# Attention block on one core: transposed maxima issued one value block sooner in the program, and the row-sum reciprocals one key tile later

## The chip, the cores and the metric

The kernel runs on one core of a Trainium2 chip. The metric is device time in microseconds for one execution; lower is better. The unchanged kernel took 2012.49 us, the median of 3 runs (2010.25 to 2014.61).

## What is computed

A transformer block: pre-norm multi-head attention with 32 heads of 20 channels over 2048 tokens of width 640, and then a gated feed-forward block. The change lies in the attention alone. Cut to that:

```python
scores = jnp.einsum("bhqd,bhkd->bhqk", q, k) * (Dh ** -0.5)
p = _softmax(scores, axis=-1)
o = jnp.einsum("bhqk,bhkd->bhqd", p, v)
h = x + o.transpose(0, 2, 1, 3).reshape(B, S, D) @ wo
h2 = h + _B_ref(_layernorm(h, axis=-1), w_gate, w_up, w_down)
```

## The kernel before, in words

The kernel has three stages: layer norm with the projections to queries, keys and values (until about 319 us in the trace), attention (until about 1443 us), and the feed-forward part. The attention is cut into 32 **units** u = 0 to 31: a group of 4 heads (g = u // 4) and a chunk of 512 queries (c = u % 4). A unit has 16 **key tiles** kt of 128 keys, so the loop runs 512 **steps**, numbered now = 16 u + kt.

A step's order is written out by hand as a string, `ORDER = "WhSmsSHMs"`, and every engine executes its own instructions in the order of the program:

- `s`, `S` (four in a step): one score product of a head on the tensor engine (PE, L1328) into a PSUM bank `ps_one`, then its exponential on ACT (L1334) into `probs`. Four banks serve `ps_one` in turn, so a bank comes round again after four uses.
- `W`: the **value block** (L1338), four products of the probabilities of two steps ago with the values, into one accumulator `acc`. Behind it stand the calls that were put off to this step (the table `later`), and one piece of `preparing`, work on the feed-forward weights (POOL copies and subtractions, loads and stores on SP; skipped at kt 3 and 4).
- `m`, `M`, `h`, `H`: score products of a *later* unit (L272), of which DVE takes the row maxima (L292, L307). The softmax subtracts these maxima inside the score product, as two extra rows of `q_stk`, so the first score product of a unit waits until the maxima have landed there.

When a unit's maxima are all there, `max_all` reduces them on DVE to `neg` (L315). How they get into `q_stk` depends on the unit. For unit 1 and the last unit of each group (v = 3, 7, ..., 31), nine times in all, `max_finish` follows: a PE transpose (L347) into a `ps_one` bank, an ACT copy and a DVE subtraction that split it in two (L89, L90), and four DMAs on SP (L354, `q_stk<-m`). For the others, POOL splits `neg` (L323, L324), DVE transposes it 4 steps later (L331), SP stores it (L332, `m_d<-turned`), and 2 steps after that SP loads it (L342, `q_stk<-m_d`).

The end of unit u - 1 lies in unit u: the last value block at kt 1, an ACT copy of the accumulator (L1348), four small DMAs that spread the row sums (L1351, `r<-o`); at the end of kt 4 the **reciprocals** on DVE (L1359), their store (L1361, `r_d<-r`) and a broadcast load of 256 KB (L1367, `rb<-r_d`); at the end of kt 9 the product `o * rb` on POOL (L1373), at the end of kt 11 four stores (L1376, `o_d<-o`). In the last two units these are earlier (kt 3, 6 and 7). At the end of kt 6 SP loads the queries of unit u + 3 (L176, `q_stk<-q_d`), and in units with c = 1 the keys, with c = 2 the values of the next group, at the end of kt 8, 10, 12 and 14 (L176, `k_stk<-k_d`; L193, `v_stk<-v_d`).

Nearly all DMAs of the attention are issued by SP, in program order. Each is given the next of eight semaphores in turn, and waits for the DMA that had it before: a DMA on SP is issued only when the eighth before it has landed.

Of the kernel before, what the change touches and what calls it, by code (L numbers as in the profile page):

```python
# [44 lines left out]
def tile_block(ctx: ExitStack, tc: tile.TileContext, x, wqkv, wo, wg, wu, wd, out):  # L45
# [42 lines left out]
    def split(src, hi, lo, lo_engine=nc.vector):  # L88
        nc.scalar.activation(hi, src, AF.Copy)  # L89
        lo_engine.tensor_tensor(out=lo, in0=src, in1=hi.bitcast(F32), op=ALU.subtract)  # L90
# [221 lines left out]
    def max_all(u):  # L312

        ends[u] = stk.tile([P, G * TPC], F32, name="neg", tag="neg", bufs=2)
        nc.vector.tensor_reduce(  # L315
            ends[u], mxs[u].rearrange("p b h t k -> p (b h t) k"), axis=AX.X, op=ALU.max, negate=True
        )
# [26 lines left out]
    def max_finish(u):  # L344

        m = (ps_one if u else ps_max)()[: G * TPC, :P]
        nc.tensor.transpose(m, ends.pop(u), ident)  # L347
        parts = stk.tile([G * TPC, 2, P], F32R, name="m2", tag="m2", bufs=1)
        split(m, parts[:, 0], parts[:, 1], nc.vector)
        for b in range(2):  # L350
            for i in range(2):
                row = b * ROW + NPART + i
                first = b * 2 * TPC
                nc.sync.dma_start(  # L354
                    queries[u][row : row + 1].bitcast(F32).rearrange(
                        "r j (t p) -> r (j t) p", t=TPC
                    ),
                    parts[first : first + 2 * TPC, i, :].bitcast(F32),
                )
# [938 lines left out]
    def weight_rings():  # L1298
        def unit(f, i):
            return lambda t: (t.rearrange("p i k n -> p (i k n)"), w_d[f][:, i])  # L1300

        def last(f):
            n = 2 if f < NF - 1 else 1
            return lambda t: (
                t[:, :, :n], w_d[f][:, 7].rearrange("p (i k n) -> p i k n", i=2, k=2)[:, :, :n]
            )

        units = stay.tile([P, 8, 2, 2, P], F32R, name="units", tag="first")
        lasts = stay.tile([P, 3, 2, 2, P], F32R, name="lasts", tag="second")
        plan = [  # L1310
            unit(f, i) for _, f in ELEMENTS for i in (range(7) if f < NF - 1 else (0, 2))
        ]
        return (
            Ring([units[:, i] for i in range(8)], plan),
            Ring([lasts[:, i] for i in range(3)], [last(f) for _, f in ELEMENTS]),
        )
# [6 lines left out]
    def scores(u, kt, j, probs):  # L1323

        p, b = divmod(j, 2)
        rows = slice(b * ROW, b * ROW + NPART + 2)
        ps = ps_one()
        nc.tensor.matmul(  # L1328
            ps,
            keys[u // NC][rows, p, kt * P : (kt + 1) * P],  # L1330
            queries[u][rows, p, :],
            start=True, stop=True,
        )
        nc.scalar.activation(probs[p][:, b, :], ps, AF.Exp, scale=scale)  # L1334
# [45 lines left out]
    todo, tail, accs, later, full, now = [], [], {}, {}, [], [0]  # L1380
    left = {u: sum(2 for a in rest if a[0] == u) for u in range(1, NU)}

    whole, halves_of = [], []

    def counted(u, n):
        left[u] -= n
# [3 lines left out]
    def next_max(b):  # L1390
        if not whole and rest:
            a = rest.pop(0)
            whole.extend((*a, i) for i in (b, 1 - b))
        if whole:
            a = whole.pop(0)
            max_one(*a)
            counted(a[0], 1)

    def next_half(b):

        if not halves_of and rest:
            a = rest.pop(0)
            halves_of.extend((i, a, []) for i in range(2))
        if not halves_of:
            return
        i, a, banks = halves_of[0]
        if not banks:
            banks.append(ps_max())
            max_half(banks[0], i, *a, b)
        else:  # L1410
            nc.tensor.keepalive_nop([nc.tensor.lower_ap(banks[0])])
            max_half(banks[0], i, *a, b)
            max_halves(banks[0], i, *a)
            counted(a[0], 2 * i)
            halves_of.pop(0)

    def weigh_next():
        u, kt, probs = todo.pop(0)
        if kt == 0:
            accs[u] = psum.tile([P, CH], F32, name="acc", tag=f"ps_{last % 3}")  # L1420
        weigh(u, kt, probs, accs[u])
        if kt == NT - 1:
            queues = [nc.sync] if u + 1 < NU else [nc.scalar, nc.sync]
            tail.append((u, *row_sums(accs.pop(u), *queues)))
# [6 lines left out]
    for u in range(NU):  # L1431
        g, c = divmod(u, NC)
        if g == NG - 1 and c >= 2:
            _, first, ln, flips, _ = ahead
            extra = [*first, *ln, lambda: None, *flips]
        for kt in range(NT):
            now[0] = u * NT + kt
            probs = [pp.tile([P, 2, CH], F32, name="probs") for _ in range(2)]
            heads = [[0, 2], [1, 3]]
            for op in ORDER if rest or whole or halves_of else LAST_ORDER:  # L1440
                if op in "mM":
                    next_max(int(op == "M"))
                elif op in "hH":
                    next_half(int(op == "H"))
                elif op in "sS":
                    scores(u, kt, heads[op == "S"].pop(0), probs)
                else:
                    if len(todo) == 2:
                        weigh_next()
                    for f in later.pop(now[0], ()):  # L1450
                        f()
                    if extra:
                        extra.pop(0)()
                    if preparing and u and kt not in (3, 4):
                        preparing.pop(0)()
                    if now[0] == (NU - NC) * NT + 8:
                        unit_ring, last_ring = weight_rings()
                        unit_ring.fill()
                        last_ring.fill()
            todo.append((u, kt, probs))  # L1460
            for v in full:
                max_all(v)
                if v % NC == NC - 1 or v == 1:
                    later.setdefault(now[0] + 2, []).append(lambda v=v: max_finish(v))
                else:
                    max_parts(v)
                    later.setdefault(now[0] + 4, []).append(lambda v=v: max_turn(v))
                    later.setdefault(now[0] + 6, []).append(lambda v=v: max_load(v))
            full.clear()
            if kt == 6 and u + 3 < NU:  # L1470
                load_queries(u + 3)
            if kt == 10 and u == 0:
                fill_ones(k_stk[1])
            if kt >= 8 and kt % 2 == 0 and c == 1 and g + 1 < NG:
                load_keys(g + 1, slice((kt - 8) // 2 * CH, (kt - 6) // 2 * CH))
            if kt >= 8 and kt % 2 == 0 and c == 2 and g + 1 < NG:
                load_values(g + 1, (kt - 8) // 2 * TPC, (kt - 6) // 2 * TPC)

            sooner = u >= NU - 2
            if kt == (3 if sooner else 4) and tail:  # L1480
                reciprocals(u - 1, tail[0][2], nc.sync)
                rb = spread(u - 1, nc.sync)
            if kt == (6 if sooner else 9) and tail:
                store_o(u - 1, tail[0][1], rb, nc.gpsimd, None)
            if kt == (7 if sooner else 11) and tail:
                store_o(u - 1, tail.pop()[1], rb, None, nc.sync)
            if g == NG - 1 and c >= 1:
                at = 8 if sooner else NT - 4
                if kt == at:
                    ahead = projection(  # L1490
                        c - 1, ps_max if c < NC - 1 else (lambda: ps_b())
                    )
                if kt in (at, at + 1, 12 if sooner else 14):
                    ahead[0][min(kt - at, 2)]()
                    if kt == at + 1 and c < NC - 1:
                        ahead[4]()
            k = 2 * (u - NU + 8)
            if kt in (12, 13) and 0 <= k + kt - 12 < ND:
                if k + kt == 12:
                    assert not preparing  # L1500
                    wo_hi = pc.tile([P, ND, D], F32R, name="wo_hi", bufs=1)
                    wo_lo = pc.tile([P, ND, D], F32R, name="wo_lo", bufs=1)
                load_wo(k + kt - 12)
            if kt in (2, 3) and 0 <= k + kt - 4 < ND:
                split_wo(k + kt - 4)
# [566 lines left out]
```

## Time and profile before

| | |
|---|---|
| median of 3 runs | 2012.49 us |
| the profiled execution | 2012.87 us, of which the span in the profile 2010.4 us |
| granted TensorE clock, mean | 0.999 |
| PE, ACT, DVE, POOL busy over the span | 99%, 72%, 80%, 39% |
| exponentials, L1334 | 2048, 612 ns each |
| reciprocals, L1359 | 32, median 243 ns |
| transposes of `max_finish` in the attention, L347 | 9, 277 ns each |

A row of the timeline gives the start, the length, the engine, the line, the operation with its output and input, and how many instructions were merged into it (a value block is eight records, two for each product); in brackets, how long the engine had been idle and what ended that. SPq stands for SP's issuing of DMAs: its length is the issue alone, not the transfer. The profile puts a wait for several semaphores down to the one that came last by its records.

### The profile page before, as it was taken

The numbers are of one execution on the slowest core, as the hardware profiler recorded it, in microseconds if no ns is written. First come the engines' busy times: TensorE is split into PE (matmuls) and PEld (weight loads), VectorE is DVE, ScalarE is ACT, GpSimd is POOL, SyncE is SP. The second block draws the span as 40 slices with busy tenths as digits, with TensorE's granted clock in tenths as the row PEclk, the third lists the DMA queues.
The fourth block names the chain that finished last, engine by engine and source line by source line (L and its number), as shares of the span: only waits on it lengthen the run. The fifth ranks groups of instructions, "written<-read, shape, count | busy, mean of one in ns | idle before, by whom it ended". The sixth has DMA issues, their size and how long they took to land. (4 is left out here: it accounts for less than half of the span.)

```text
span 2010.4 us, 41923 instructions
## 1 busy us (share of the span) xinstructions
PE 1985.1 (99%) x14794; PEld 1268.7 (63%) x14794; DVE 1599.5 (80%) x2831; ACT 1440.1 (72%) x2827; POOL 789.4 (39%) x1182
## 2 busy tenths in 40 slices
PE   8999999999999999999999999999999999999998
PEld 6999995444444444444444444455598888888887
DVE  5687778899999899998999999975477666676667
ACT  4678778999999999999999999987633222212221
POOL 7464424343453443443400011011155544844465
PEclk9999999999999999999999999999999999999999
DMA  7887563443634544435412132222268655974642
GB/s 244 255 258 257 183 206 78 128 140 105 193 103 141 152 135 138 157 127 175 150 60 68 40 86 58 79 63 62 62 215 278 228 168 174 359 248 160 203 146 93
DMA packets 199350, 310.48 MB, mean 154 GB/s; under 512 B 53744, under 2 KB 87856, under 8 KB 198120
## 3 DMA queue, kind: packets, MB, share of 16 engines
q1 hardware_dynamic: 192552, 284.21, 44.0%
q0 software_dynamic: 6496, 23.60, 4.0%
q8 instruction: 120, 1.97, 0.4%
q14 instruction: 86, 0.70, 0.1%
q10 hardware_dynamic: 96, 0.00, 0.0%
HBM read 208.11 MB, written 99.19 MB: 153 GB/s over the span
## 5 line engine op out<-in xcount | busy, mean ns | idle before, releaser
L1334 ACT ACTIVATE probs<-ps_one 128x512 f32<-128x512 f32 x2048 | 1056.1, 612 | 46.7 <-PE ps_one L1328 37.2
L292 DVE TENSOR_REDUCE mx<-ps_max 128x1 f32<-128x512 f32 x980 | 671.8, 686 | 90.6 <-PE ps_max L272 88.0
L272 PEld LDWEIGHTS ps_max<-k_stk,q_stk 60*128 60x128 f32 x1964 | 294.2, 185 | 462.8 <-DVE mx L307 393.5
L1328 PE MATMUL ps_one<-q_stk,k_stk 62*128 62x512 f32 x2048 | 570.4, 427 | 2.7 <-DMA q_stk<-m 1.8
L272 PE MATMUL ps_max<-k_stk,q_stk 60*128 60x256 f32 (+1 forms) x1964 | 565.5, 376 | 2.5 <-DVE mx L292 1.2
L1338 PE MATMUL acc<-probs,v_stk 128*32 128x512 f32 x4096 | 546.1, 605 | 0.1
L307 DVE TENSOR_REDUCE mx<-ps_max 128x2 f32<-128x512 f32 x492 | 335.8, 683 | 0.4 <-PE ps_max L272 0.4
L1328 PEld LDWEIGHTS ps_one<-q_stk,k_stk 62*128 62x128 f32 x2048 | 304.9, 184 | 15.0 <-ACT probs L1334 11.3
L1750 DVE TENSOR_TENSOR tmp<-ps_a,tmp 128x512 f32<-128x512 f32 x208 | 141.3, 690 | 122.2 <-PE ps_a L1535 96.6
L262 DVE TENSOR_REDUCE mx<-ps_max 128x2 f32<-128x512 f32 x288 | 180.8, 685 | 63.7 <-PE ps_max L240 60.2
L252 ACT ACTIVATE ps_max<-ps_max 128x512 f32<-128x512 f32 x288 | 151.6, 583 | 42.9 <-PE ps_max L240 40.3
L1629 PE MATMUL ps_b<-halves,yp 128*128 128x320 f32 x1032 | 179.0, 308 | 1.5 <-DMA halves<-j_d 1.3
L1629 PEld LDWEIGHTS ps_b<-halves,yp 128*128 128x128 f32 x1032 | 165.2, 188 | 17.5 <-POOL yp L90 1.5
L1535 PE MATMUL ps_a<-t,units 128*128 128x512 f32 x624 | 162.5, 396 | 0.0
L1338 PEld LDWEIGHTS acc<-probs,v_stk 128*32 128x32 f32 x4096 | 80.7, 108 | 128.1 <-issue 119.9
L90 POOL TENSOR_TENSOR yp<-y,yp 128x256 fp32r<-128x256 f32 x96 | 60.2, 628 | 189.7 <-ACT yp L89 189.7
L1535 PE MATMUL ps_a<-z,units 128*128 128x512 f32 x516 | 133.8, 394 | 0.0
L1535 PEld LDWEIGHTS ps_a<-t,units 128*128 128x128 f32 x624 | 112.6, 188 | 18.5
L1373 POOL TENSOR_TENSOR o<-o,rb 128x512 f32<-128x512 f32 x31 | 39.8, 1284 | 194.2 <-DMA rb<-r_d 60.6
L1634 DVE TENSOR_TENSOR h<-ps_b,h 128x320 f32<-128x320 f32 x248 | 110.1, 482 | 6.8 <-PE ps_b L1629 5.4
L671 PE MATMUL ps_one<-z_hi,w_lo 64*128 64x512 f32 x380 | 113.4, 392 | 0.0
L671 PE MATMUL ps_one<-z_lo,w_hi 64*128 64x512 f32 x380 | 112.1, 392 | 0.0
(228 smaller groups left out, 2746.5 us busy)
## 6 DMA issues: line engine op xcount, KB each, us to landing
units<-w_d SPq DMA_DIRECT2D x186, 256.0 KB
w_d<-stage SPq DMA_DIRECT2D x106, 256.0 KB
halves<-j_d SPq DMA_DIRECT2D x70, 320.0 KB
j_d<-stage SPq DMA_DIRECT2D x42, 320.0 KB
k_stk<-k_d SPq DMA_DIRECT2D x64, 160.0 KB
q_stk<-q_d SPq DMA_DIRECT2D x64, 160.0 KB
raw<-k_d SPq DMA_DIRECT2D x62, 160.0 KB
raw<-q_d SPq DMA_DIRECT2D x54, 160.0 KB
```

Source lines behind the costliest of these rows:

```text
L252: nc.scalar.activation(ps, ps, AF.Relu)
L262: nc.vector.tensor_reduce(mx[:, b, :, t, kc], ps.rearrange("p (j n) -> p j n", j=2), axis=AX.X, op=ALU.max,)
L272: nc.tensor.matmul(ps, queries[u][rows, pair, t * P : (t + 1) * P], keys[u // NC][rows, pair, k0:k1], start=True, stop=True, skip_group_ch ...
L292: nc.vector.tensor_reduce(mx[:, b, pair, t, kc : kc + 1], ps, axis=AX.X, op=ALU.max)
L307: nc.vector.tensor_reduce(max_slots(u)[:, :, pair, t, slot], ps.rearrange("p (j n) -> p j n", j=2), axis=AX.X, op=ALU.max,)
L671: nc.tensor.matmul(ps, a[rows], b[rows], start=(i == n == 0), stop=(i == 1 and n == last), skip_group_check=True,)
L1328: nc.tensor.matmul(ps, keys[u // NC][rows, p, kt * P : (kt + 1) * P], queries[u][rows, p, :], start=True, stop=True,)
L1334: nc.scalar.activation(probs[p][:, b, :], ps, AF.Exp, scale=scale)
L1338: nc.tensor.matmul(acc[32 * j : 32 * j + 32, :], values[u // NC][:, kt, j * VW : j * VW + 32], probs[j // 2][:, j % 2, :], start=(kt == 0) ...
L1535: nc.tensor.matmul(ps.rearrange("p (t n) -> p t n", t=TPC), w[k][:, i], z[k][:, :, j], start=(first and m == 0), stop=(last and m == len(n ...
L1629: nc.tensor.matmul(ps, a, b, start=(n == 0), stop=(n == len(pairs) - 1))
L1750: add = lambda out, ps, x: nc.vector.tensor_tensor(out=out, in0=ps, in1=x, op=ALU.add)
```

## The change

Two edits in the step loop. First, `max_finish` is no longer put into the table for the `W` of two steps after the maxima were complete, where it stood behind the value block. It goes into a list that is emptied at the end of the next step, so its transpose, copy, subtraction and four DMAs come ahead of the following value block. Second, in units 1 to 29 the reciprocals, their store and the broadcast load come at the end of kt 5 and not of kt 4. The products and stores that use them stay at kt 9 and 11.

```diff
-    whole, halves_of = [], []
+    whole, halves_of, behind_step = [], [], []
...
             todo.append((u, kt, probs))
+            while behind_step:
+                behind_step.pop(0)()
             for v in full:
                 max_all(v)
                 if v % NC == NC - 1 or v == 1:
-                    later.setdefault(now[0] + 2, []).append(lambda v=v: max_finish(v))
+                    behind_step.append(lambda v=v: max_finish(v))
                 else:
...
             sooner = u >= NU - 2
-            if kt == (3 if sooner else 4) and tail:
+            if kt == (3 if sooner else 5) and tail:
                 reciprocals(u - 1, tail[0][2], nc.sync)
                 rb = spread(u - 1, nc.sync)
```

On PE, around the first transpose (for unit 1, in step 13 of unit 0; L1338 is the value block, L347 the transpose, L1328 scores, L272 products for maxima), the program before has:

```order
L1328 MATMUL ps_one<-q_stk,k_stk_125 128x512 x2
L272 MATMUL ps_max<-k_stk_125,q_stk 128x256
L272 MATMUL ps_max<-k_stk_125,q_stk 128x512
L1328 MATMUL ps_one<-q_stk,k_stk_125 128x512
L1338 MATMUL acc<-probs,v_stk_126 32x512 x4
L347 MATMUL ps_one<-ident,neg 16x128
L272 MATMUL ps_max<-k_stk_125,q_stk 128x256
```

and the changed one:

```order
L1328 MATMUL ps_one<-q_stk,k_stk_125 128x512 x2
L272 MATMUL ps_max<-k_stk_125,q_stk 128x256
L272 MATMUL ps_max<-k_stk_125,q_stk 128x512
L1328 MATMUL ps_one<-q_stk,k_stk_125 128x512
L347 MATMUL ps_one<-ident,neg 16x128
L1338 MATMUL acc<-probs,v_stk_126 32x512 x4
L272 MATMUL ps_max<-k_stk_125,q_stk 128x256
```

Only the transpose and the value block change places; so it is for eight of the nine. The ninth (unit 31) moves ahead of four score products as well, and there the ACT copy also moves ahead of other work. ACT is otherwise unchanged, and POOL's order is unchanged throughout.

On SP, in unit 9, from the row-sum DMAs to the load of the next unit's maxima (w_d is a store of prepared weights), before:

```order
L1351 DMA r<-o 32x1x16 x4
L1137 DMA w_d_84<-stage 128x512 x2
L1361 DMA r_d<-r 4x32x16
L1367 DMA rb<-r_d 128x1x512
L1137 DMA w_d_84<-stage 128x512 x2
L176 DMA q_stk<-q_d_59 40x1024
```

and changed:

```order
L1351 DMA r<-o 32x1x16 x4
L1137 DMA w_d_84<-stage 128x512 x3
L1361 DMA r_d<-r 4x32x16
L1367 DMA rb<-r_d 128x1x512
L1137 DMA w_d_84<-stage 128x512
L176 DMA q_stk<-q_d_59 40x1024
```

One weight store now stands ahead of the pair `r_d<-r`, `rb<-r_d`. Everything behind keeps its order: three more query loads, a weight store, two weight loads, four key loads, the store of the turned maxima, four key loads, the load of the maxima. In unit 10, whose maxima take the other path, the end of the row reads before:

```order
L1376 DMA o_d<-o 20x512 x4
L1137 DMA w_d_86<-stage 128x512
L193 DMA v_stk_5606<-v_d 128x4x96
L354 DMA q_stk<-m_11431 1x8x128 x4
L1137 DMA w_d_86<-stage 128x512 x2
```

and changed:

```order
L1376 DMA o_d<-o 20x512 x4
L1137 DMA w_d_86<-stage 128x512
L354 DMA q_stk<-m_11424 1x8x128 x4
L193 DMA v_stk_5606<-v_d 128x4x96
L1137 DMA w_d_86<-stage 128x512 x2
```

The four DMAs of the maxima are issued ahead of a load of values. The same exchange is made in units 2, 6, 14, 18, 22 and 26.

On DVE the reciprocal moves past three reductions in every unit. In 15 of the units it then stands directly behind `neg` (L315), as here in unit 5, before:

```order
L292 TENSOR_REDUCE mx_7745<-ps_max 128x1
L1359 RECIPROCAL r<-r 128x16
L285 MEMSET mx_8446 128x16x2
L292 TENSOR_REDUCE mx_8446<-ps_max 128x1
L307 TENSOR_REDUCE mx_7745<-ps_max 128x2
L292 TENSOR_REDUCE mx_8446<-ps_max 128x1
L315 TENSOR_REDUCE neg<-mx_7745 128x16
L292 TENSOR_REDUCE mx_8446<-ps_max 128x1
```

and changed:

```order
L292 TENSOR_REDUCE mx_7745<-ps_max 128x1
L285 MEMSET mx_8442 128x16x2
L292 TENSOR_REDUCE mx_8442<-ps_max 128x1
L307 TENSOR_REDUCE mx_7745<-ps_max 128x2
L292 TENSOR_REDUCE mx_8442<-ps_max 128x1
L315 TENSOR_REDUCE neg<-mx_7745 128x16
L1359 RECIPROCAL r<-r 128x16
L292 TENSOR_REDUCE mx_8442<-ps_max 128x1
```

## The prediction

> **What bounds the kernel now.** I read the page's first lines, then the attention by engine in order of time, step by step, then SP's row.
>
> ```profile
> span 2010.4 us, 41923 instructions
> PE 1985.1 (99%) x14794; PEld 1268.7 (63%) x14794; DVE 1599.5 (80%) x2831; ACT 1440.1 (72%) x2827; POOL 789.4 (39%) x1182
> ```
>
> PE is busy 99% of the span. What the change can touch are the steps of the attention that are longer than PE's own work. An ordinary step, and one with a transpose, on PE:
>
> ```profile
> 345.44 1.06 PE L1338 MATMUL acc<-probs,v_stk 128*32 128x512 f32 x8
> 346.44 0.38 PE L272 MATMUL ps_max<-k_stk,q_stk 60*128 60x256 f32 x1
> 347.14 0.39 PE L1328 MATMUL ps_one<-q_stk,k_stk 62*128 62x512 f32 x1
> 347.51 1.07 PE L1338 MATMUL acc<-probs,v_stk 128*32 128x512 f32 x8
> 348.51 0.28 PE L347 MATMUL ps_one<-ident,neg 128*16 128x128 f32 x1
> 348.71 0.38 PE L272 MATMUL ps_max<-k_stk,q_stk 60*128 60x256 f32 x1
> 349.52 0.49 PE L1328 MATMUL ps_one<-q_stk,k_stk 62*128 62x512 f32 x1
> 349.94 0.64 PE L1338 MATMUL acc<-probs,v_stk 128*32 128x512 f32 x4
> ```
>
> The ordinary step lasts 347.51 - 345.44 = 2.07 us: 1.00 for the value block and 1.07 for the products behind it. The step with the transpose lasts 349.94 - 347.51 = 2.43, which is 0.36 more: 0.20 for the transpose and 0.16 in the products.
>
> **Edit 1, on PE.** Who frees the transpose's bank, and who holds it:
>
> ```profile
> 346.36 1.21 ACT L1334 ACTIVATE probs<-ps_one 128x512 f32<-128x512 f32 x2
> 348.90 0.25 ACT L89 ACTIVATE m<-ps_one 16x128 fp32r<-16x128 f32 x1
> 349.19 0.28 DVE L90 TENSOR_TENSOR m<-ps_one,m 16x128 fp32r<-16x128 f32 x1 [0.20 <-ACT m L89]
> ```
>
> The transpose takes the bank of the step's first score, whose exponential (the second in the first row) ends at 346.36 + 1.21 = 347.57. The 0.16 lies at the other end: the last score of the next set takes the transpose's bank back, and starts at 349.52, just 0.05 after DVE's subtraction ends (349.19 + 0.28 = 349.47). In the changed order the transpose can start at 347.57 + 0.05 = 347.62; this wait of 0.11 (from 347.51) was hidden behind the value block and is now in the open. Then value block at 347.82, first product at 348.82, and the last score 0.70 behind it, as in the ordinary step (347.14 - 346.44): at 349.52, which is when the bank is free. The step ends at 348.82 + 1.07 = 349.89 and not at 349.94: **0.05 less**. The ACT copy stays behind four exponentials, and with it the subtraction. Bounds: 0.16 gained if the subtraction holds nothing up, 0.20 lost if copy and subtraction slip by the transpose's own time. Eight transposes are of this kind; three of them fall in units whose next start waits for DMAs (below), so 5 x 0.05 = **-0.25**. The ninth, among the output projection, I take as nothing (at most 0.3 either way, about the size of such a step's excess).
>
> **Edit 2, on DVE.** Two reciprocals stop DVE, and PE after it:
>
> ```profile
> 400.29 1.06 PE L1338 MATMUL acc<-probs,v_stk 128*32 128x512 f32 x8
> 400.75 0.25 DVE L1359 RECIPROCAL r<-r 128x16 f32<-128x16 f32 x1 [1.07 <-DMA r<-o]
> 403.22 0.64 PE L1338 MATMUL acc<-probs,v_stk 128*32 128x512 f32 x4
> 670.89 0.25 DVE L1359 RECIPROCAL r<-r 128x16 f32<-128x16 f32 x1 [1.55 <-DMA r<-o]
> ```
>
> The first (unit 2) makes a step of 403.22 - 400.29 = 2.93 us, 0.86 over 2.07. In the second (unit 10) DVE waits 1.55 - 1.07 = 0.48 longer, so I put it at 1.34. One key tile later DVE reaches the reciprocal 2.07 us later, more than it waited: both stalls go. **-0.86** in unit 2; the 1.34 of unit 10 is given back, as SP's row will show.
>
> In 15 units the reciprocal now directly follows `neg`.
>
> ```profile
> 346.23 0.68 DVE L292 TENSOR_REDUCE mx<-ps_max 128x1 f32<-128x512 f32 x1
> 346.83 0.23 DVE L315 TENSOR_REDUCE neg<-mx 128x16 f32<-128x80 f32 x1
> ```
>
> A maximum takes 0.60 from its start to that of the next (346.83 - 346.23); three take 1.80 of 2.07, and 0.27 is free. `neg` and reciprocal want some 0.20 each, 0.03 less than they last, so DVE falls 0.13 behind, once. PE feels that only where a bank comes back late. The longest held is that of the step's last maximum: it is read out at 346.91 (346.23 + 0.68), and PE wants it again for a product beside the last score, at 347.14 or later: some 0.2 to spare. So I take nothing; were nothing to spare, 15 x 0.13 = 2.0 lost.
>
> **Edit 2, on SP.** This is the large term. SP in unit 9, POOL's product there, and the start of unit 10 on PE:
>
> ```profile
> 637.65 0.58 SPq L1367 DMA_DIRECT2D rb<-r_d  x1
> 638.28 0.94 SPq L1137 DMA_DIRECT2D w_d<-stage  x2
> 639.26 1.60 SPq L176 DMA_DIRECT2D q_stk<-q_d  x4
> 640.91 0.35 SPq L1137 DMA_DIRECT2D w_d<-stage  x1
> 644.14 0.40 SPq L1166 DMA_DIRECT2D raw<-in_B_w_gate  x1
> 644.43 1.29 POOL L1373 TENSOR_TENSOR o<-o,rb 128x512 f32<-128x512 f32 x1 [5.04 <-ACT probs L1334]
> 653.99 2.79 SPq L342 DMA_DIRECT2D q_stk<-m_d  x4
> 657.77 0.38 PE L272 MATMUL ps_max<-k_stk,q_stk 60*128 60x256 f32 x1
> 658.23 0.47 PE L1328 MATMUL ps_one<-q_stk,k_stk 62*128 62x512 f32 x1
> ```
>
> The broadcast load `rb` goes out at 637.65. Seven DMAs follow; the eighth, at 644.14, stands until `rb` has landed, 6.5 us after its issue, and POOL's product starts then too. Behind it SP goes on, up to the maxima, which are all issued at 653.99 + 2.79 = 656.78. Unit 10's first score is due beside the product at 657.77 and comes at 658.23: it waits for them. Move the reciprocal by 2.07, and `r_d`, `rb` and all behind move with it, less the weight store that now goes ahead (0.94 / 2, about 0.5): the start of unit 10 comes **1.5 later**. The start of unit 18, behind unit 17 with the same row of DMAs, is late too:
>
> ```profile
> 929.93 0.38 PE L272 MATMUL ps_max<-k_stk,q_stk 60*128 60x256 f32 x1
> 930.99 0.47 PE L1328 MATMUL ps_one<-q_stk,k_stk 62*128 62x512 f32 x1 [0.68 <-DMA q_stk<-m_d]
> ```
>
> Its first score is 1.06 behind the product, and I add the same **+1.5**. The other units with c = 1 come out early enough today, and I take it that their room holds this.
>
> A page of the Trainium skill would shrink this term. "DMA: Bandwidth & Descriptors", Anatomy of one DMA, fits a DMA (on GpSimd's queue) by 2.0 us plus bytes over 436 GB/s; for 256 KB that is an estimate of 2.6 us and not 6.5, SP would not stand at the eighth DMA, and the sum would be that of the first rival. In this stretch the rows decide against it: 644.14 - 637.65.
>
> **Both edits, at the starts of units 11, 15 and 19,** whose maxima take the other path:
>
> ```profile
> 684.58 0.73 POOL L1178 TENSOR_TENSOR sums<-raw 128x256 f32<-128x256 f32 x1 [20.96 <-DMA raw<-in_B_w_up]
> 690.32 0.43 SPq L193 DMA_DIRECT2D v_stk<-v_d  x1
> 690.85 2.82 SPq L354 DMA_DIRECT2D q_stk<-m  x4
> 693.38 0.38 PE L272 MATMUL ps_max<-k_stk,q_stk 60*128 60x256 f32 x1
> 694.96 0.47 PE L1328 MATMUL ps_one<-q_stk,k_stk 62*128 62x512 f32 x1 [1.20 <-DMA q_stk<-m]
> 829.07 0.38 PE L272 MATMUL ps_max<-k_stk,q_stk 60*128 60x256 f32 x1
> 829.64 0.47 PE L1328 MATMUL ps_one<-q_stk,k_stk 62*128 62x512 f32 x1 [0.18 <-ACT probs L1334]
> 960.92 0.61 SPq L193 DMA_DIRECT2D v_stk<-v_d  x1
> 961.62 2.84 SPq L354 DMA_DIRECT2D q_stk<-m  x4
> ```
>
> Unit 11's first score is 694.96 - 693.38 = 1.58 late, at the end of a chain: weight loads behind `rb`, POOL's sums that wait for them (684.58), the product, the four stores of `o`, a weight store, the value load, the maxima. Edit 1 takes the value load out: 690.85 - 690.32 = 0.53. Edit 2 moves the weight loads. DVE comes to unit 10's reciprocal at 670.89 - 1.55 = 669.34 today, and with a late start and one key tile more at 669.34 + 1.5 + 2.07 = 672.9, which is 2.0 after 670.89; less 0.5 for the store ahead, 1.5. So the maxima go out 1.5 - 0.53 = 1.0 later, and as they, not PE, set the start of unit 11, units 10 and 11 together lose **+1.0**: the 1.5 at unit 10's start and the 1.34 saved in it both end in this wait. Unit 15 is 0.57 late. There the first weight load stands seventh behind `rb` in the changed order and no longer waits for it, and the value load is out of the way: I take 0.35, the part over the 0.2 that other first steps cost, **-0.35**. Unit 19 has unit 11's chain: loads 1.5 later, less 961.62 - 960.92 = 0.7 for the value load, **+0.8**.
>
> **Sum.** -0.25 - 0.86 + 1.5 + 1.0 - 0.35 + 0.8 = +1.8. The profiled execution took 2012.87 (span 2010.4 and 2.5 around it), 0.4 above the median of 2012.49. It comes to 2014.7; from the median 2014.3, and I say **2014.3**.
>
> **Rivals.** *SP's delay is taken up* (faster): if `rb`, with one store fewer behind it, lands sooner, or SP's pauses take up the shift, no start is later, the reciprocals' stalls stay saved (0.86 + 1.34), and edit 1 brings forward three starts (0.53, 0.35, 0.7) and five steps (0.25): -4.0, so 2008.5 from the median. For it: SP pauses between 640.91 and 644.14. Against: that pause ends with `rb` itself. Chance 0.22. The page's short DMA gives this time. The same page's Rules for kernel authors, to issue a DMA early and wait late, speak for edit 1 and against edit 2.
>
> *The whole 2.07 arrives* (slower): if the weight store ahead of `r_d` frees nothing, because the row is paced by landings, unit 18 loses 2.07, unit 11's chain 2.07 + 0.5 - 0.53 = 2.0, unit 15 2.07 - 0.53 = 1.5 and unit 19 1.4. With -0.25 - 0.86 that is +5.9, so 2018.4. It decides as soon as the DMAs behind `rb` go out over 1.8 us later. Chance 0.20.
>
> *Edit 1 does not do what it says*: if PE meets the bank later than I reckon, each of eight steps is 0.20 longer and not 0.05 shorter, +1.6 + 0.25 on the sum, 2016.2. Chance 0.08. The forecast has 0.50.
>
> **Range and chances.** From the faster rival's time, but for its lower half, to just over the slower one's: 2008.8 to 2019.0. A measurement of this kernel can tell about 0.2%, or 4 us, from no change. Faster than 2008.5: half of the first rival and a little, 0.14. Slower than 2016.5: the second rival and a tail of the forecast, 0.25. Between: 0.61.
>
> **What would show it.** Transposes ahead of their value block, in steps of about 2.38; no DVE idle ahead of a reciprocal; `rb` issued some 2 us later in its unit, and POOL's product with it; unit 18's first score 2.5 behind its product, not 1.06; unit 15's not late. If `q_stk<-m_d` in units 9 and 17 goes out no later than now, the large term is wrong, and the time falls to the first rival's.

## The result, and the profile after

The changed kernel took **2018.13 us** (median of 6 runs, 2016.5 to 2020.21), the kernel before, beside it, 2012.54 (6 runs, 2010.25 to 2016.11). The ratio is 1.0028, with a 95% interval of 1.0018 to 1.0038: slower, by 5.6 us. The time lies within the predicted range, but 3.8 above the forecast, and next to the second rival's 2018.4. It is over 2016.5, where the prediction had put a chance of 0.25, and not in its likeliest band of 2008.5 to 2016.5, with 0.61.

The page's first lines; the busy times of the engines are nearly those of before, only the span is longer:

```profile
span 2016.1 us, 41908 instructions
PE 1985.5 (98%) x14794; PEld 1267.4 (63%) x14794; DVE 1599.1 (79%) x2831; ACT 1440.1 (71%) x2827; POOL 789.4 (39%) x1182
```

So most of the 5.7 us (2016.1 - 2010.4) must be waiting. The waits of PE at scores, before, and after (total, times, longest):

```profile
PE ps_one L1328 <- DMA q_stk<-m: 1.8, 2, 1.2
PE ps_one L1328 <- DMA q_stk<-m_d: 0.7, 1, 0.7
```

```profile
PE ps_one L1328 <- DMA q_stk<-m_d: 4.4, 3, 2.4
PE ps_one L1328 <- DMA q_stk<-m: 3.1, 3, 1.2
PE ps_one L1328 <- DVE m L90: 0.9, 1, 0.9
```

PE waits for maxima at the start of six units instead of three, and 5.0 us longer (4.4 + 3.1 - 2.5); at a transposed pair of maxima it waits for the first time, 0.9. The timeline of PE in the changed kernel has each of these places; the products (L272) at unit starts stand ahead of the waiting score, as in the rows of before:

```profile
655.97 1.06 PE L1338 MATMUL acc<-probs,v_stk 128*32 128x512 f32 x8
656.96 0.38 PE L272 MATMUL ps_max<-k_stk,q_stk 60*128 60x256 f32 x1
659.76 0.47 PE L1328 MATMUL ps_one<-q_stk,k_stk 62*128 62x512 f32 x1 [2.42 <-DMA q_stk<-m_d]
660.91 1.93 PE L1338 MATMUL acc<-probs,v_stk 128*32 128x512 f32 x8
664.30 1.06 PE L1338 MATMUL acc<-probs,v_stk 128*32 128x512 f32 x8
...
797.33 0.47 PE L1328 MATMUL ps_one<-q_stk,k_stk 62*128 62x512 f32 x1 [0.47 <-DMA q_stk<-m_d]
832.66 0.47 PE L1328 MATMUL ps_one<-q_stk,k_stk 62*128 62x512 f32 x1 [1.17 <-DMA q_stk<-m]
934.88 0.47 PE L1328 MATMUL ps_one<-q_stk,k_stk 62*128 62x512 f32 x1 [1.50 <-DMA q_stk<-m_d]
969.78 0.47 PE L1328 MATMUL ps_one<-q_stk,k_stk 62*128 62x512 f32 x1 [0.73 <-DMA q_stk<-m]
1388.14 0.50 PE L1328 MATMUL ps_one<-q_stk,k_stk 62*128 62x512 f32 x1 [0.92 <-DVE m L90]
```

These are the starts of units 10, 14, 15, 18 and 19 (unit 11 waits 1.20, as before), and in unit 30 the score that wants the bank of the last transposed maxima. Unit 10's first score comes 659.76 - 656.96 = 2.80 behind its product, where it was 0.46. And the next step, from 660.91 to 664.30, takes 3.39 us instead of some 2.1: its value block is 1.93 long, where those around it take 1.06. The stretches around it, with the granted clock in the third column from the right:

```profile
656.00:660.00 4.00, 1.58 (x12) 0.57 (x13) 1.43 (x3) 1.50 (x4) 3.68 (x9) 1.00 0.13 29
660.00:662.00 2.00, 2.00 (x15) 0.68 (x13) 1.69 (x3) 1.73 (x4) 1.84 (x5) 0.63 0.51 131
662.00:664.00 2.00, 2.00 (x12) 1.22 (x8) 0.38 (x2) 1.33 (x3) 1.84 (x5) 0.52 0.67 146
664.00:668.00 4.00, 4.00 (x34) 1.59 (x33) 3.59 (x6) 3.92 (x9) 0.73 (x1) 1.00 0.87 297
```

The clock fell behind PE's pause and came back some 4 us later. What SP did ahead of that pause (unit 9; the time is that of issuing):

```profile
637.07 0.60 SPq L1361 DMA_DIRECT2D r_d<-r  x1
639.06 0.57 SPq L1367 DMA_DIRECT2D rb<-r_d  x1
642.22 0.42 SPq L1166 DMA_DIRECT2D raw<-in_B_w_gate  x1
645.67 0.38 SPq L1166 DMA_DIRECT2D raw<-in_B_w_up  x1
649.48 0.35 SPq L332 DMA_DIRECT2D m_d<-turned  x1
655.54 2.78 SPq L342 DMA_DIRECT2D q_stk<-m_d  x4
```

and the two rows of before that the prediction did not show:

```profile
635.63 0.61 SPq L1361 DMA_DIRECT2D r_d<-r  x1
648.31 0.35 SPq L332 DMA_DIRECT2D m_d<-turned  x1
```

Whole traces are shifted against each other by earlier waits, so I measure SP's DMAs back from unit 10's first product (657.77 before, 656.96 after). The store of reciprocals went out 22.14 us ahead of it and now 19.89, the broadcast load 20.12 and now 17.90, the store of the turned maxima 9.46 and now 7.48, their load 3.78 and now 1.42. So everything is late by 2.0 to 2.4, and nothing was taken up. One weight load (642.22) no longer stands for the broadcast load, as the prediction had it for unit 14, but the next one (645.67) does, 6.6 us after `rb` was issued.

The steps of the attention, summed by unit (from the value block at kt 0 of a unit to that of the next, each read from the starts of L1338's rows; one execution of each kernel):

| place | predicted | measured |
|---|---|---|
| transposes ahead of the value block | -0.25 | 0.0 |
| unit 2 | -0.86 | -0.17 |
| units 10 and 11 together | +1.0 | +2.06 |
| unit 14 | 0 | +0.79 |
| unit 15 | -0.35 | +0.97 |
| unit 18 | +1.5 | +0.82 |
| unit 19 | +0.8 | +0.15 |
| unit 30 | 0 | +0.56 |
| whole attention | +1.8 | +5.0 |

The other 0.7 of the span lie in parts that the change doesn't touch: the attention began 0.53 sooner, and what follows it took 1.21 longer.

### The profile page after: what moved, and what is told of

Its sections match the earlier page's. It is cut to its first block, busy times and chain, and to the rows that moved or that the text cites. A ratio compares the mean times of both kernels' runs of the same rounds, so it can differ in the third digit from the quotient of the medians.

```text
span 2016.1 us, 41908 instructions
## 1 busy us (share of the span) xinstructions
PE 1985.5 (98%) x14794; PEld 1267.4 (63%) x14794; DVE 1599.1 (79%) x2831; ACT 1440.1 (71%) x2827; POOL 789.4 (39%) x1182
## 5 line engine op out<-in xcount | busy, mean ns | idle before, releaser
L272 PEld LDWEIGHTS ps_max<-k_stk,q_stk 60*128 60x128 f32 x1964 | 294.2, 185 | 468.1 <-DVE mx L307 399.8
L1328 PE MATMUL ps_one<-q_stk,k_stk 62*128 62x512 f32 x2048 | 569.2, 427 | 8.4 <-DMA q_stk<-m_d 4.4
L272 PE MATMUL ps_max<-k_stk,q_stk 60*128 60x256 f32 (+1 forms) x1964 | 566.0, 376 | 1.5 <-DVE mx L262 1.0
L1338 PE MATMUL acc<-probs,v_stk 128*32 128x512 f32 x4096 | 547.0, 606 | 0.0
L1328 PEld LDWEIGHTS ps_one<-q_stk,k_stk 62*128 62x128 f32 x2048 | 304.1, 185 | 21.0 <-ACT probs L1334 10.7
L1338 PEld LDWEIGHTS acc<-probs,v_stk 128*32 128x32 f32 x4096 | 80.8, 108 | 126.8 <-issue 118.1
```

What stands on the lines that cost most here:

```text
L272: nc.tensor.matmul(ps, queries[u][rows, pair, t * P : (t + 1) * P], keys[u // NC][rows, pair, k0:k1], start=True, stop=True, skip_group_ch ...
L1328: nc.tensor.matmul(ps, keys[u // NC][rows, p, kt * P : (kt + 1) * P], queries[u][rows, p, :], start=True, stop=True,)
L1338: nc.tensor.matmul(acc[32 * j : 32 * j + 32, :], values[u // NC][:, kt, j * VW : j * VW + 32], probs[j // 2][:, j % 2, :], start=(kt == 0) ...
```

## The experiments

**Theory:** the cost is edit 2 on SP. SP stands at the store of the reciprocals until DVE has made them; a key tile later for DVE is a key tile later for each DMA behind, up to the maxima of the next unit. **Rivals:** edit 1 costs a part; the reciprocal's new place on DVE, or the late product on POOL, costs a little in every unit; or it is the new order of SP's row and not its time. The first four runs were timed beside each other (kernel before: 2011.57, 33 runs).

**Edit 1 alone.** From the changed kernel:

```diff
-            if kt == (3 if sooner else 5) and tail:
+            if kt == (3 if sooner else 4) and tail:
```

Expected:

> Edit 1 alone: maxima turned ahead of the value block, reciprocals back at kt 4. Theory (SP stands at the store of the reciprocals, and everything behind goes out 2 us later): the cost goes away, and what is left is edit 1's own: first scores of units 11, 15 and 19 earlier by 0.5, 0.35 and 0.7 us, unit 30 longer by 0.5 (its last score waits for the transposed maxima's bank), steps with a transpose unchanged in sum, DVE stalls in units 2 and 10 back: about 1 us faster than before, 2011.5. Rival (edit 1 costs a part of the 5.6 us, as its wait is now in the open): slower than before by 1 us or more, with longer starts than before in units 11, 15, 19.

Measured: 2011.06, ratio 0.9995 (0.9985 to 1.0006). Edit 1 costs nothing that can be told. In the trace the starts of units 11 and 15 are 0.5 sooner each, unit 30 loses 0.56, and the steps with transposes give back 0.0. Unit 19 is 0.13 sooner and not 0.7, and unit 18 takes 0.71 longer although unit 17's reciprocals are at kt 4: 0.29 of it in its first step, 0.42 where its own reciprocal waits.

**Edit 2 alone.** The kernel before, with the reciprocals at kt 5:

```diff
-            if kt == (3 if sooner else 4) and tail:
+            if kt == (3 if sooner else 5) and tail:
```

Expected:

> Edit 2 alone: reciprocals at kt 5, maxima turned behind the value block. Theory: all of the loss and a little more, since the value loads are again ahead of the maxima: first score of unit 10 late by over 2.4 us, units 14, 15, 18 late as in the changed kernel or by 0.5 more, no long wait in unit 30: 5 to 7 us slower than before. Rival (the loss comes from both edits together): 2 to 4 us slower.

Measured: 2019.97, ratio 1.0035 (1.0024 to 1.0047): 7.0 us by the ratio and 8.4 by the medians, where 5 to 7 were expected. The whole loss is edit 2's. In the traces edit 1 takes some of it back (the attention is 8 longer than before here, 5 with both); the ratios don't tell the two kernels apart. Three of the starts (units 11, 15 and 18):

```profile
696.27 0.47 PE L1328 MATMUL ps_one<-q_stk,k_stk 62*128 62x512 f32 x1 [1.66 <-DMA q_stk<-m]
697.26 1.82 PE L1338 MATMUL acc<-probs,v_stk 128*32 128x512 f32 x8
834.14 0.47 PE L1328 MATMUL ps_one<-q_stk,k_stk 62*128 62x512 f32 x1 [1.46 <-DMA q_stk<-m]
936.47 0.76 PE L1328 MATMUL ps_one<-q_stk,k_stk 62*128 62x512 f32 x1 [1.67 <-DMA q_stk<-m_d]
938.23 1.08 PE L1338 MATMUL acc<-probs,v_stk 128*32 128x512 f32 x4
```

With the value load still ahead of them, units 11 and 18 are later than in the changed kernel (1.66 and 1.67), and there too a long value block follows, 1.82 for eight records and 1.08 for four (0.64 elsewhere). Units 10 and 11 lose 4.2 together, 14 and 15 2.0, 18 and 19 3.0; no other unit loses more than 0.1.

**Where it sits.** The changed kernel with kt 5 in units of c = 0 and 3 alone:

```diff
-            if kt == (3 if sooner else 5) and tail:
+            if kt == (3 if sooner else 5 if c in (0, 3) else 4) and tail:
```

Expected:

> The changed kernel, but with the reciprocals at kt 5 only in units with c = 0 and c = 3, and at kt 4 in those with c = 1 and c = 2. Theory: the later reciprocal costs only where the maxima's DMAs come late behind it, which is in c = 1 and c = 2, so this equals edit 1 alone within 0.5 us. Rival (the cost is in every unit, as by the reciprocal's new place behind the negated maxima on DVE, which half of these 15 places keep, or by POOL's later product): about half of the 5.6 us stays, 2.5 us slower than before.

Measured: 2011.43, ratio 0.9995 (0.9984 to 1.0006): as edit 1 alone. Half the reciprocals are moved, at no cost that shows. The cost sits in units with c = 1 and 2, in which SP also loads keys or values, and a cost of each moved reciprocal on DVE or POOL is out.

**The reciprocal's time, or the row's order?** The changed kernel with the reciprocal on DVE back at kt 4, its two DMAs at kt 5, so SP's order is that of the changed kernel:

```diff
+            if kt == 4 and tail and not sooner:
+                reciprocals(u - 1, tail[0][2], None)
+                halfway[u - 1] = True
```

Called without a queue, `reciprocals` makes the reciprocal alone; at kt 5 it then issues the store alone.

Expected:

> The changed kernel with the reciprocal on DVE back at kt 4, but its store and broadcast load left at kt 5 in SP's order. It keeps the changed order of SP's row and takes away only the later time of the reciprocal. Theory (the time counts, not the order): SP finds the reciprocal done, the store goes out within 0.5 us of where it was before, unit 10's first score is late by less than 1 us, and the time is that of edit 1 alone within 1 us. Rival (the new order of the row costs, with a weight store and in some units weight loads ahead of the pair): the starts stay late and it is 3 to 6 us slower than before.

Measured: 2009.16, ratio 0.9980 (0.9971 to 0.9990). The cost is gone, and with the new order the time is 1.9 below edit 1 alone: unit 11's start is 1.54 sooner than before, unit 15's 0.56, unit 19's 0.94. So it is the time at which SP gets past the store of reciprocals, not the row's order. Not all came as expected: the time is more than 1 us below edit 1 alone, and in this trace unit 10's first score is still 1.15 behind its product, where it was 0.46 before.

The next four were timed together too (kernel before: 2012.56, 27 runs).

**SP relieved of the pair.** The changed kernel, reciprocals at kt 5, but their store and the broadcast load issued from GpSimd's queue:

```diff
-                reciprocals(u - 1, tail[0][2], nc.sync)
-                rb = spread(u - 1, nc.sync)
+                own_queue = nc.sync if sooner else nc.gpsimd
+                reciprocals(u - 1, tail[0][2], own_queue)
+                rb = spread(u - 1, own_queue)
```

Expected:

> The changed kernel, but in units 1 to 29 the store of the reciprocals and the broadcast load are issued from GpSimd's queue at the end of kt 5, so that no DMA behind them on SP stands for DVE's reciprocal. If the cost is SP standing at that store (the theory), the starts of units 10, 11, 14, 15, 18 and 19 come back and the time falls to that of edit 1 alone or below it, 2009 to 2012, although the reciprocal itself is still one key tile late. If the cost is in the reciprocal's place on DVE, or in the later product on POOL, it stays at 2016 to 2020. GpSimd's own issuing could add something to POOL's work, below 2 us in all.

Measured: 2009.46, ratio 0.9982 (0.9973 to 0.9991). GpSimd's rows, SP's of the same stretch, and unit 10's first product:

```profile
636.62 0.70 POOL L1361 DMA_DIRECT2D r_d<-r  x1 [0.48 <-DVE mx L292]
644.57 1.29 POOL L1373 TENSOR_TENSOR o<-o,rb 128x512 f32<-128x512 f32 x1 [3.59 <-DMA rb<-r_d]
...
644.47 0.35 SPq L332 DMA_DIRECT2D m_d<-turned  x1
650.09 2.81 SPq L342 DMA_DIRECT2D q_stk<-m_d  x4
...
655.68 0.38 PE L272 MATMUL ps_max<-k_stk,q_stk 60*128 60x256 f32 x1
```

The store of the reciprocals is even later than in the changed kernel (19.06 ahead of the product, against 19.89), and POOL's product still waits for `rb`; but the store of the turned maxima is 11.2 ahead, their load 5.6, and no unit start waits for `q_stk<-m_d`. So the reciprocal's lateness alone costs nothing. Nor does SP's standing alone, and there my theory was too simple: SP stands here too, and longer than in the changed kernel, at a weight store that waits for POOL's work (total, times, longest; 630 to 660 us):

```profile
SPq L1137 <- POOL stage L1147: 9.2, 2, 9.0
```

In the changed kernel the longest wait there is 6.8, at the store of the reciprocals. The difference is what follows: here the weight store goes out at 641.01 and the maxima's store 3.46 behind it, as nothing on SP waits for `rb`; in the changed kernel the maxima's store goes out 10.42 behind `rb`.

**Twice the delay.** The changed kernel with the reciprocals at kt 6:

```diff
-            if kt == (3 if sooner else 5) and tail:
+            if kt == (3 if sooner else 6) and tail:
```

Expected:

> The changed kernel with the reciprocals, their store and the broadcast load yet another key tile later, at the end of kt 6 in units 1 to 29. By the theory (SP stands at the store until the reciprocal is done, and all behind it is shifted) each start that is already late for DMAs is later by about another 2 us: units 10, 14, 15, 18 and 19 together with what they hand on give 8 to 12 us more, 2026 to 2030. If the cost came once, from the new order in SP's row or from the clock after a pause, it stays at 2017 to 2021.

Measured: 2014.50, ratio 1.0010 (1.0001 to 1.0018). Here my theory fell: twice the delay costs about a third. SP's row of unit 9 and unit 10's start:

```profile
638.26 0.60 SPq L1361 DMA_DIRECT2D r_d<-r  x1
640.26 0.57 SPq L1367 DMA_DIRECT2D rb<-r_d  x1
641.88 0.60 SPq L1166 DMA_DIRECT2D raw<-in_B_w_up  x1
646.99 0.35 SPq L332 DMA_DIRECT2D m_d<-turned  x1
653.89 2.77 SPq L342 DMA_DIRECT2D q_stk<-m_d  x4
...
656.22 0.38 PE L272 MATMUL ps_max<-k_stk,q_stk 60*128 60x256 f32 x1
658.09 0.47 PE L1328 MATMUL ps_one<-q_stk,k_stk 62*128 62x512 f32 x1 [1.49 <-DMA q_stk<-m_d]
659.07 1.48 PE L1338 MATMUL acc<-probs,v_stk 128*32 128x512 f32 x8
```

The store of reciprocals is indeed another 1.93 us later (17.96 ahead of the product). But at kt 6 a fourth weight store and the four loads of queries stand ahead of it in the program, and go out while SP would otherwise wait. So there are fewer DMAs behind `rb`, neither weight load stands (641.88 is the second), and the eighth behind it is the store of the turned maxima itself, at 646.99, when `rb` lands. That store is 9.23 ahead of the product, against 7.48 with kt 5 and 9.46 before. So the theory is to be mended: SP's delay at one DMA is not handed on as a whole; what counts is **when the maxima's store gets through, and that hangs on the landing of `rb` and on how many DMAs stand between the two**. Even so it doesn't give unit 10's start here, 1.87 behind its product with a store only 0.23 later than before. The load behind the store waits for its landing (`SPq L342 <- DMA m_d<-turned` in the list of waits), and went out 6.90 after it, where it was 5.68 before; with the reciprocal at kt 4 and the DMAs at kt 5 it was 6.71. What makes that landing longer I did not settle.

**Unit 9 alone.** The kernel before with kt 5 in unit 9 only:

```diff
-            if kt == (3 if sooner else 4) and tail:
+            if kt == (3 if sooner else 5 if u == 9 else 4) and tail:
```

Expected:

> The kernel before with edit 2 in unit 9 alone (kt 5 there, kt 4 everywhere else). By the theory the start of unit 10 alone is late, by 2.0 to 3.2 us at its first step, and where PE stands over 2 us at that place the next step is 1.1 to 1.3 us long at a granted clock near 0.5; 1.3 come back in unit 10, whose reciprocal no longer waits, and unit 11's start differs by less than 0.5. The starts of units 14, 15, 18 and 19 are within 0.3 us of the kernel before. If the clock drop had nothing to do with the pause, the second step would keep its length.

One execution: 2013.24. In its trace:

```profile
399.03 0.24 DVE L1359 RECIPROCAL r<-r 128x16 f32<-128x16 f32 x1
...
659.43 0.47 PE L1328 MATMUL ps_one<-q_stk,k_stk 62*128 62x512 f32 x1 [2.56 <-DMA q_stk<-m_d]
660.41 1.93 PE L1338 MATMUL acc<-probs,v_stk 128*32 128x512 f32 x8
```

One moved reciprocal in unit 9 gives the whole picture of unit 10: the first step 2.47 longer, the next 1.45 with its value block of 1.93, 1.35 given back at unit 10's reciprocal; 2.24 for the unit, -0.43 for unit 11, and units 14 to 19 within 0.1 of before. The first row is a second finding: unit 2 is unchanged in this kernel, and its reciprocal doesn't wait at all, where the one execution of before that I read had it wait 1.07. That stall comes and goes between executions.

**Unit 31.** The run with the reciprocal at kt 4 and its DMAs at kt 5, with unit 31's maxima put behind the value block as before:

```diff
-                    behind_step.append(lambda v=v: max_finish(v))
+                    if v == NU - 1:
+                        later.setdefault(now[0] + 2, []).append(lambda v=v: max_finish(v))
+                    else:
+                        behind_step.append(lambda v=v: max_finish(v))
```

Expected:

> The run with the reciprocal on DVE at kt 4 and its two DMAs at kt 5 of SP's row, and the maxima of unit 31 behind the value block as before. The theory: the 0.56 us that unit 30 lost in every kernel with edit 1 goes, so 0.5 us less than that run had against its kernel before: a ratio of 0.9975, about 2008.5. If the excess in unit 30 has another cause, the ratio stays at 0.998.

Measured: 2008.66, ratio 0.9984 (0.9975 to 0.9993). In the trace the 0.56 is gone (unit 30 within 0.02 of before); the ratio can't tell a change of that size, and its value went the other way.

The last two were timed beside 15 runs of the kernel before (2013.74).

**The mended theory, put to use.** As the last, but the pair of DMAs at kt 6, the reciprocal on DVE still at kt 4:

```diff
-            if kt == (3 if sooner else 5) and tail:
+            if kt == (3 if sooner else 6) and tail:
```

Expected:

> Both edits but the reciprocal on DVE at kt 4, its store and broadcast load at kt 6 of SP's row, and the maxima of unit 31 behind the value block as before. The corrected theory says that what counts is when the store of the turned maxima gets through on SP, and that is set by the wait for the broadcast load and by how many DMAs stand between: here the store of the reciprocals goes out as early as with kt 5 (the reciprocal is done by then), while the weight stores, and the four queries, are already ahead of it, so the row no longer stands at the weight loads. Starts of units 10, 11, 15, 18 and 19 all at most 0.3 late, time 2007.0 to 2008.7. The uncorrected theory (only the time of the reciprocal counts) gives the time of the run with kt 5, 2008.7. If the later broadcast load makes POOL's product late, units lose at the accumulators' end and the time rises over 2010.

Measured: **2006.87** (2006.23 to 2007.89), ratio 0.9964 (0.9952 to 0.9977), just under the time expected: faster than both kernels, and the lowest ratio here, though its interval still touches those of the runs at 0.9980 to 0.9985. SP's row of unit 9, and unit 10's start:

```profile
634.79 0.59 SPq L1367 DMA_DIRECT2D r_d<-r  x1
643.29 0.35 SPq L332 DMA_DIRECT2D m_d<-turned  x1
649.43 2.76 SPq L342 DMA_DIRECT2D q_stk<-m_d  x4
...
657.01 0.38 PE L272 MATMUL ps_max<-k_stk,q_stk 60*128 60x256 f32 x1
657.01 0.49 PE L1328 MATMUL ps_one<-q_stk,k_stk 62*128 62x512 f32 x1
```

The store of reciprocals is as early as before (22.22 ahead of the product), the maxima's store 13.72 and their load 7.58. The load again goes out 6.14 after the store, but now there is room for it. The first score stands beside its product: no start waits for maxima any more.

**The pair on GpSimd's queue, and unit 31 as before** (the same edit as for unit 31 above, made to the run with GpSimd's queue).

Expected:

> The run with the pair on GpSimd's queue, and the maxima of unit 31 behind the value block as before. That run lost 1.9 us in unit 30 in its profile, most of it in a step of 5.18 us in which the granted clock fell to 0.50. If the transpose ahead of the value block is what loses it, this run takes 0.6 to 1.9 us less, 2007.5 to 2008.9; if the loss comes from elsewhere in that unit, 2009.5 again.

Measured: 2009.90, ratio 0.9985 (0.9976 to 0.9994). Inconclusive: unit 30 is within 0.05 of before in this trace, so the 1.9 of the other went with the transpose's place or with that one execution; the ratios (0.9982 and 0.9985) can't tell.

## Why the prediction was right in kind and short in size

It named the mechanism, the row on SP in unit 9, and the place, the start of unit 10. But its forecast had a part of SP's delay swallowed there, and in other units all of it, and this failed. The second rival's condition, DMAs behind `rb` over 1.8 us later, is met: 2.2 for `rb` and 2.0 for the maxima's store. Its total is right to 0.3 us, though not through its own terms: it gave unit 18 2.07 and unit 19 1.4, which lost 0.82 and 0.15, and left out unit 14, the slow clock and unit 30. So its closeness is luck. Of the signs that the prediction named, the transpose's step, the later `rb` and POOL's product with it (2.56 later against unit 10's product) came as said; unit 18's first score is 1.88 behind its product and not 2.5, unit 15's is 1.55 late, and DVE still waits once ahead of a reciprocal. Step by step:

- **"less the weight store that now goes ahead (0.94 / 2, about 0.5)"** failed in unit 9. The row is not paced by issuing but by `rb`'s landing, so a store less behind `rb` frees only its own place in the count of eight: one weight load passed, the next stood in its stead. Unit 10's first step lost 2.49, not 1.5.
- **Unit 10's second step** was not in the sum at all: +1.26 from the granted clock. With -0.32 in the step after it and -1.35 at the reciprocal that waits no more (1.34 predicted), unit 10 lost 2.05, and unit 11, whose start waits 1.20 as before, handed on nothing. So "units 10 and 11 together lose +1.0" measured +2.06: the first step was 0.99 longer than reckoned and the slow clock added 0.94 (1.26 - 0.32), while what unit 11 was to lose (1.0 - 1.5 + 1.34 = 0.84) did not come.
- **"The other units with c = 1 come out early enough today, and I take it that their room holds this"** failed in unit 13: unit 14 waits 0.47 and loses 0.79. Here I had not read the room; it was a row away.
- **Unit 15, -0.35:** measured +0.97. Its first weight load passes but the second stands for `rb`, as in unit 9, and the chain goes on from there. Edit 1 alone gave -0.49 there.
- **Unit 18, +1.5,** measured +0.82, and **unit 19, +0.8,** +0.15: both too high. In unit 17 `rb` is 2.2 later, as in unit 9, but the store of the maxima only 0.55 and their load 0.96 (each against unit 18's first product). From `rb` to that store it took 11.6 before and now 9.9; which of the waits between gave way I did not settle. Nor is the 0.82 clearly edit 2's, since edit 1 alone has 0.71 there in its one trace.
- **Unit 2, -0.86:** the stall there is not of this kernel but of one execution; the unit-9 run and edit 1 alone, both with the reciprocal at kt 4 in unit 2, don't have it. In the changed kernel's trace the four row-sum DMAs were issued later, the reciprocal waited 0.91 one step later, and -0.17 was left. A wait read in one execution was priced as if it were in each.
- **Transposes, 5 x -0.05:** measured 0.0. The step with the transpose and the one behind it took 4.50 before (347.51 to 349.94 and the ordinary 2.07) and take 4.50 now. PE's rows in the changed kernel:

```profile
344.86 1.06 PE L1338 MATMUL acc<-probs,v_stk 128*32 128x512 f32 x8
347.04 0.28 PE L347 MATMUL ps_one<-ident,neg 128*16 128x128 f32 x1
347.25 1.06 PE L1338 MATMUL acc<-probs,v_stk 128*32 128x512 f32 x8
349.36 1.06 PE L1338 MATMUL acc<-probs,v_stk 128*32 128x512 f32 x8
```

  The transpose's step is 347.25 - 344.86 = 2.39 (2.38 predicted), but the next, which I took for an ordinary one, is 349.36 - 347.25 = 2.11 and not 2.07.
- **The ninth transpose,** put at nothing with 0.3 either way, is +0.56 or more in every trace with edit 1 in unit 31, and within 0.05 in every one without: the score behind it waits 0.92 for DVE's subtraction.
- **DVE's 15 pairs of `neg` and reciprocal, put at nothing,** are right: units 3 to 9 are each within 0.1 of before.

## What to carry to other kernels

On an in-order queue, an instruction that waits delays all behind it, so put such a DMA where its input is long ready, and let independent DMAs go ahead of it: beside edit 1 alone the same two DMAs cost some 6 us with a late input, and gained some 6 with an early one and a later place (ratios of 1.0028 and 0.9964 against 0.9995, the second with unit 31 as before). With a fixed number of transfers in flight, count which DMA stands as the eighth behind a slow one; here, moving a DMA over that border mattered more than a microsecond or two on the queue. And before a stall is booked as a saving, look whether a second execution has it.

## What the runs showed of the hardware

A short pause of PE can halve its clock. In these traces, pauses of 1.49, 1.66, 1.67, 2.42, 2.56 and 2.94 us at a unit's start each ran into a stretch with a granted clock of 0.50; pauses of 1.20, 1.36, 1.46 and 1.50 did not. In the changed kernel the loss is (1 - 0.63) x 2 + (1 - 0.52) x 2 = 1.70 us of clock, which at half speed is a stretch of 3.4 us, and it lengthened the steps by 1.26.

The Trainium skill, "TensorE: Matmul & The Clock Gate", Part 1, tells of a gate that halves the clock after an idle window of about 3.4 us, and gives it back after a busy one as long. The length of the slow stretch agrees; the pause that sets it off at a unit's start is shorter here, 1.5 us and more.

Why 1.49 did and 1.50 did not, the traces show in part. Each slow stretch in the attention lasts 3.41 us, and where a trace has several, the next begins a whole number of such lengths behind the end of the one before: 660.51 - 326.00 = 334.51, or 98 x 3.4133, in the changed kernel; 334.51, 34.13 (10 x 3.4133) and 235.52 (69 x 3.4133) with edit 2 alone. So it looks as if PE were judged in stretches of that length whose borders don't move with its pauses. Counted on from 663.92, a border lies at 663.92 + 79 x 3.4133 = 933.57, within the pause of 1.50 that ends at 934.88, so that no stretch has more than 1.31 of it; the pause of 1.49 lies in one stretch whole (656.60 to 658.09, the slow one beginning at 659.58). This is read from the traces, not tried.

The pause's length is not all, either: the clock also fell to 0.50 at the attention's start (323.21 to 326.62 in the kernel before, and in ten of the twelve traces), where no pause is over 1.0, and in unit 30 of the run with GpSimd's queue, with no such pause ahead of it. These runs don't show why.
